# A fused RWKV scan and Sinkhorn MoE: the fallback becomes a loop over time steps, and its flag and branch move ahead of the decay table

## The chip, the cores and the metric

The kernel runs on one core of one Trainium2 chip. The metric is device time in microseconds (us), the median of several executions; lower is better. Engines are named as the profile names them: PE (TensorE matmul) and PEld (its weight load), DVE (VectorE), ACT (ScalarE), POOL (GpSimd) and SP (SyncE, which here only issues DMAs). A small q behind an engine's name means its sequencer, the part that reads instructions, waits for semaphores, branches and issues DMAs.

## What is computed

An attention-like recurrence with a decay per head and channel (B, H, S, D = 4, 8, 768, 48), whose output goes through a mixture of experts (3072 tokens, 384 wide, 8 experts of 1024) with gate weights that are normalised over rows and columns eight times. Cut to what matters:

```python
def _attn_ref(r, k, v, w, u):
    state = np.zeros((B, H, D, D), dtype=np.float32)
    for t in range(S):
        kt, vt, rt = (k[:, :, t], v[:, :, t], r[:, :, t])
        cur = np.einsum('bhd,bhe->bhde', u[None] * kt, vt)
        y[:, :, t] = np.einsum('bhd,bhde->bhe', rt, state + cur)
        state = w[None, :, :, None] * state + np.einsum('bhd,bhe->bhde', kt, vt)

def _moe_ref(x, w_gate, w1, w2):
    logits = x @ w_gate
    P = np.exp(logits - logits.max())
    for _ in range(8):
        P /= P.sum(1, keepdims=True) + 1e-09
        P /= P.sum(0, keepdims=True) + 1e-09
        P *= N / E
    for e in range(E):
        out += P[:, e:e + 1] * (np.maximum(x @ w1[e], 0.0) @ w2[e])
```

The decay w is drawn from 0.85 to 0.95.

## The kernel before

The scan is done in chunks of 128 time steps. Inside a chunk the powers of w are factored into r and k, so that a chunk is matmuls; a table of the powers (the decay table) is built once at the start. It works while w lies in [0.7, 1.1]. Channels outside of that are masked out of the table, and for them there is a fallback, scan_channels, which runs the recurrence channel by channel. Whether it runs is decided on the chip: a flag, the maximum over "w differs from w clamped", is loaded into a register of each engine (`nc.values_load`, L444), and an `If` (L445) jumps over the fallback when it is zero, as it is with the inputs above.

The program is fully unrolled, and the order on each engine is the order of the code: the wrapper `InOrder` (L21) keeps each engine's instructions as they are written, and records them all under L29, so groups in the profile are told apart by the tiles they write and read. The flag's load and the branch are not wrapped: where they fall among an engine's instructions is the framework's decision. Tiles of the pool `ps3` (L258, tag "pa") share four PSUM buffers in rotation: the fifth tile of the tag waits until the first is read out.

The start of the program, in order:

- w is loaded twice as `wt` (L264, L265; one half by SP, one by ACT's queue) for the table, and once as `wrow` (L266, ACT's queue) for the flag. SP loads r and k of token tiles 0 and 1 (`rn`, `kn`, L291).
- Fills: `hbx`, a third each on POOL, DVE and ACT (L305 to L313), then small ones on POOL.
- PE multiplies zeros (`spin`, tile `pz`) so that its clock is up when work comes: 25 matmuls (L314).
- DVE builds the decay table: `wsafe`, the scan `pw`, the flag's three instructions (L327 to L329), the reciprocal `iv`, two products `tab`. ACT copies two parts (`tabr`). PE transposes eight blocks (`pt_tab`, L342), and ACT copies them out as `rtab` and `ktab`. DVE writes `wc` and `wbd` from the table.
- The flag's load and the branch over the fallback.
- 8 more spins (L449). SP loads v of tile 0, `ub`, r and k of tile 2 (in the program as built these four stand ahead of SP's branch), then the first expert's weight w1 in three pieces (tile `ws`, L458), then tiles further on.

Behind that each token tile goes through prep (POOL: `rp` = rn times rtab; DVE: `kp` = kn times ktab), stage_b (transposes `prT`, `pkT` on PE, copies on ACT), stage_c (`pA` = kT by rT; DVE copies it under a mask to `at`; `pu`, from which DVE makes the state `S`), stage_d (`py`, then `x` on DVE) and the transposes and gate logits behind it. Five spins stand after stage_b and after stage_c while there is no expert work to put there. On DVE `wm`, the maximum of the first expert's w1 in three pieces, is placed among the tiles' instructions: its first piece stands between kp of tile 2 and `dg` and `at` of tile 0. From tile 5 on PE fills the gaps with the first expert's matmuls (`ph`, `po`), and from there to the end it is the experts that are computed.

The fallback before is a loop over the 4 batches (L384); in its body the 4 pairs of heads and 48 channel steps of each are unrolled. DVE's part of it is about 1,260 rows of the program, PE's about 1,620, SP's about 80.

## Time and profile before

| | |
|---|---|
| median of 3 runs | 1607.49 us (1604.43 to 1607.59) |
| the profiled execution's own time | 1602.74 us |
| its span on the core | 1601.0 us |
| PE busy | 1571.7 us, 98% |
| DVE, ACT, POOL busy | 1019.0, 668.6, 587.9 us |
| mean granted clock of PE | 0.995 |
| share of the chain that ended last on PE | 93% |
| PE busy in 0 to 10, 10 to 20, 20 to 30 us | 7.79, 3.79, 10.00 us |
| PE busy in 40 to 100 us, by tens | 9.32, 9.48, 8.46, 8.85, 7.70, 10.00 us |

The span runs from the first instruction on the core to the last; the execution's time has some 1.7 us around it. Busy time of PE counts the spins too, which compute nothing. In a row of the timeline stand the start, the duration, engine, line, operation, the tile written and the tiles read, how many instructions are merged, and in brackets how long the engine had stood idle and what released it.

### The profile page before, as it was taken

The page shows a single profiled execution, that of the slowest core. Times are in us where ns is not written, and L with a number is a line of the kernel's source. Part 1 is how long each engine was busy: PE and PEld are TensorE (multiplying, and loading weights), DVE is VectorE, ACT ScalarE, POOL GpSimd, SP SyncE. Part 2 cuts the span into 40 slices and gives each one's busy share as a digit, 9 for nine tenths or more (in the row PEclk, how much of TensorE's full clock was granted, in tenths as well). Part 3 has the DMA queues.
Part 4 walks back from the last instruction along what each step waited for, and adds up shares of the span by engine and source line. Part 5 has one row for each costly group of instructions (what it writes and reads, how often), then busy time and mean ns, then how long its engine had stood idle before and what let it go on. Part 6 is the DMA issues. An engine that isn't in the chain of part 4 may idle for free.

```text
span 1601.0 us, 24304 instructions
## 1 busy us (share of the span) xinstructions
PE 1571.7 (98%) x9433; PEld 909.6 (57%) x9433; DVE 1019.0 (64%) x1706; ACT 668.6 (42%) x1190; POOL 587.9 (37%) x688
## 2 busy tenths in 40 slices
PE   7999999999999999999999999999999999999999
PEld 5778777555455555555555555555555555555555
DVE  6776665675766666666666666666665666656554
ACT  2333333343444444454535454544444453535320
POOL 6567674442021343434243424243332424242200
PEclk8999999999999999999999999999999999999999
DMA  7333230212022567566666656664545554545434
GB/s 180 63 69 85 66 86 26 92 42 84 35 94 54 104 85 124 74 123 85 124 84 100 110 74 123 85 113 55 95 55 94 58 96 54 94 56 89 60 89 133
DMA packets 163899, 136.60 MB, mean 85 GB/s; under 512 B 88257, under 2 KB 158018, under 8 KB 163778
## 3 DMA queue, kind: packets, MB, share of 16 engines
q0 software_dynamic: 44928, 61.36, 31.6%
q1 hardware_dynamic: 118640, 73.63, 15.9%
q8 instruction: 75, 1.23, 0.3%
q14 instruction: 46, 0.38, 0.1%
q10 hardware_dynamic: 210, 0.00, 0.0%
HBM read 53.69 MB, written 80.22 MB: 84 GB/s over the span
## 4 chain that ended last, share of the span: by engine, by line
PE 93%; DVE 3%; POOL 1%; issue 1%; ACT 1%; ACTq 0%; DVEq 0%; POOLq 0%
PE po L29 46%; PE bZ L29 11%; PE bY L29 11%; PE ph L29 5%; PE bB L29 4%; PE bA L29 4%; PE py L29 4%; PE bC L29 2%; PE pA L29 1%; PE pu L29 1%; POOL tb L29 1%; PE pz L29 1%; PE prT L29 1%; PE pkT L29 1%; PE px L29 0%
## 5 line engine op out<-in xcount | busy, mean ns | idle before, releaser
L29 PE MATMUL po<-ws,hbx 128*128 128x384 f16 x3360 | 736.9, 326 | 0.0
L29 POOL DMA_DIRECT2D accd<-stg x288 | 250.4, 870 | 701.2 <-ACT stg L29 682.8
L29 PEld LDWEIGHTS <-hbx 128*128 128x128 f16 x3576 | 336.9, 98 | 287.4
L29 PEld LDWEIGHTS <-ws 128*128 128x128 f16 x3096 | 302.8, 98 | 248.2 <-issue 6.3
L29 ACT ACTIVATE hbx<-tb 128x512 f16<-128x512 f32 x224 | 141.5, 632 | 443.5 <-DVE tb L29 443.5
L29 PE MATMUL po<-ws,hb 128*128 128x384 f16 x1248 | 322.2, 327 | 3.2 <-DVE ws L29 2.3
L29 DVE TENSOR_TENSOR tb<-bY,tb 128x512 f32<-128x512 f32 x168 | 116.2, 692 | 194.4 <-PE bY L29 193.3
L29 ACT ACTIVATE stg<-po,pe 128x384 f32<-128x384 f32 x312 | 179.6, 575 | 128.0 <-PE po L29 102.5
L29 PE MATMUL bZ<-xv,ws 128*128 128x512 f16 x840 | 227.0, 379 | 0.7 <-DVE tb L29 0.6
L29 PE MATMUL bY<-xv,ws 128*128 128x512 f16 x840 | 227.0, 379 | 0.1
L29 DVE TENSOR_TENSOR tb<-bZ,tb 128x512 f32<-128x512 f32 x168 | 115.5, 688 | 132.9 <-PE bZ L29 132.9
L29 PEld LDWEIGHTS <-hb 128*128 128x128 f16 x1248 | 122.1, 98 | 96.4 <-issue 4.7
L29 POOL TENSOR_TENSOR ucb<-rawb 128x256 f32<-128x256 f32 x84 | 75.5, 949 | 93.1 <-DMA rawb<-in_moe_w_dram 66.7
L29 DVE TENSOR_TENSOR tb<-bB,tb 128x512 f32<-128x512 f32 x112 | 77.5, 692 | 49.6 <-PE bB L29 47.7
L29 PE MATMUL ph<-hbx,ws 128*128 128x384 f16 x576 | 103.9, 328 | 1.3 <-DVE hb L29 1.2
L29 DVE SCALAR_TENSOR_TENSOR hbx<-tb,hbx 128x512 f16<-128x512 f32 x112 | 78.0, 696 | 24.3 <-ACT hbx L29 19.5
L29 DVE SCALAR_TENSOR_TENSOR hb<-tb,hbx 128x512 f16<-128x512 f32 x112 | 77.2, 689 | 24.7 <-ACT hbx L29 19.5
L29 PE MATMUL bA<-xv,ws 128*128 128x512 f16 x336 | 90.8, 379 | 1.0 <-ACT tb L29 1.0
L29 PE MATMUL bB<-xv,ws 128*128 128x512 f16 x336 | 90.8, 379 | 0.0
L29 DVE SCALAR_TENSOR_TENSOR hb<-ph,hb 128x384 f16<-128x384 f32 x64 | 35.5, 555 | 59.0 <-ACT hb L29 58.8
L29 ACT COPY tb<-bZ 128x512 f32<-128x512 f32 x56 | 32.8, 586 | 68.1 <-PE bZ L29 68.1
L29 ACT ACTIVATE hb<-ph 128x384 f16<-128x384 f32 x64 | 31.5, 492 | 58.0 <-PE ph L29 56.7
(163 smaller groups left out, 1645.0 us busy)
## 6 DMA issues: line engine op xcount, KB each, us to landing
accd<-stg POOLq DMA_DIRECT2D x288, 192.0 KB, 3.7
rawb<-in_moe_w_dram SPq DMA_DIRECT2D x28, 768.0 KB, 7.3
e0d<-stg SPq DMA_DIRECT2D x48, 192.0 KB, 1.9
hb<-e0d SPq DMA_DIRECT2D x48, 192.0 KB, 3.5
rn<-in_r_dram SPq DMA_DIRECT2D x24, 192.0 KB, 3.1
kn<-in_k_dram SPq DMA_DIRECT2D x24, 192.0 KB, 3.5
vn<-in_v_dram SPq DMA_DIRECT2D x24, 192.0 KB, 2.8
accd<-stg SPq DMA_DIRECT2D x24, 192.0 KB, 1.8
```

Source lines behind the costliest of these rows:

```text
L29: return lambda *a, **k: self.tc.keep_in_program_order(f(*a, **k))
```

## The change

- The fallback becomes a short loop over the 768 time steps: it holds the state of 48 by 48 per batch and head with one partition per value channel, and each step is a handful of DVE instructions and seven DMAs. Its scratch tiles lie in `hbx` instead of `ws1`, `hb3` and PSUM. It has no PE instructions.
- The flag's load of w goes first on ACT's queue, its three DVE instructions stand right behind the fills and ahead of the table, and load and branch are written ahead of the table's code, without `high_priority`.
- The table's code (wsafe to wbd) stands behind SP's loads in the text. POOL's fills, mask and wbd, that followed it, stand before it.
- 25 spins before and 8 after the branch become 19 before it, 5 ahead of the table's transposes and 4 behind them.

```diff
+    wr = w.rearrange("(p two) d -> two d p", two=2)
+    S_.dma_start(wrow, w.rearrange("(o h) d -> o h d", o=1))
     V.memset(wt, 1.0)
-    wr = w.rearrange("(p two) d -> two d p", two=2)
     Q.dma_start(wt[:D, :], wr[0])
     S_.dma_start(wt[HP : HP + D, :], wr[1])
-    S_.dma_start(wrow, w.rearrange("(o h) d -> o h d", o=1))
...
-    spin(25)
-    wsafe = ac.tile([P, NPAIR], F32, name="wsafe")
...
-    V.tensor_scalar(wlim, wrow, W_MAX, W_MIN, op0=ALU.min, op1=ALU.max)
-    V.tensor_tensor(wlim, wlim, wrow, op=ALU.not_equal)
-    V.tensor_reduce(flag, wlim, axis=AX.XY, op=ALU.max)
-    V.reciprocal(iv, pw)
...
+    spin(19)
     wbd = ac.tile([P, NPAIR, 2, D], F32, name="wbd")
     G.memset(wbd, 0.0)
...
+    V.tensor_scalar(wlim, wrow, W_MAX, W_MIN, op0=ALU.min, op1=ALU.max)
+    V.tensor_tensor(wlim, wlim, wrow, op=ALU.not_equal)
+    V.tensor_reduce(flag, wlim, axis=AX.XY, op=ALU.max)
...
-        with tc.For_i(0, B, 1) as b:
-            for a in range(NPAIR):
...
-                for e in range(D):
...
+        with tc.For_i(0, S, 1) as t:
+            for dst, src in ((kb, k), (rb, r)):
+                Q.dma_start(
+                    dst,
+                    src.rearrange("b h s d -> s (b h) d")[bass.ds(t, 1)].broadcast_to([D, BH, D]),
+                )
+            Q.dma_start(vt, v.rearrange("b h s d -> s d (b h)")[bass.ds(t, 1)].rearrange("o d a -> (o d) a"))
+            V.tensor_tensor(rb, rb, stt, op=ALU.mult)
+            V.tensor_reduce(yv, rb, axis=AX.X, op=ALU.add)
...
+            V.tensor_tensor(of_b(stt), of_b(stt), for_b(wz), op=ALU.mult)
+            V.tensor_tensor(stt, stt, kv, op=ALU.add)
...
-    with tc.high_priority():
-        bad = nc.values_load(flag.bitcast(I32), min_val=0, max_val=0x3F800000)
-        with tc.If(bad > 0):
-            with tc.tile_pool(name="scratch", bufs=1, space=bass.MemoryType.DRAM) as scratch:
-                scan_channels(scratch)
-
-    spin(8)
+    bad = nc.values_load(flag.bitcast(I32), min_val=0, max_val=0x3F800000)
+    with tc.If(bad > 0):
+        with tc.tile_pool(name="scratch", bufs=1, space=bass.MemoryType.DRAM) as scratch:
+            scan_channels(scratch)
+
...
+    spin(5)
+    for src, dst in ((tab, rtab), (tabr, ktab)):
+        pt = ps3.tile([P, NPAIR, P], F32, tag="pa", name="pt_tab")
...
+        S_.copy(dst.rearrange("p a j d -> p a (j d)"), pt)
+    spin(4)
```

What this does to the order on the engines. On DVE, behind the last fill, with `hb_73` standing for the memory in which wrow, wlim, pw, iv and tab lie:

```order
+L29 TENSOR_SCALAR hb_73<-hb_73 1x384
+L29 TENSOR_TENSOR hb_73<-hb_73 1x384
+L29 TENSOR_REDUCE flag<-hb_73 1x1
+L384 TENSOR_LOAD flag
 L29 TENSOR_SCALAR wsafe<-wt 128x4
 L29 COPY hb_73<-wsafe 128x4x64
 L29 SCALAR_TENSOR_TENSOR hb_73<-hb_73 128x260
 L29 TENSOR_TENSOR good<-wt,wsafe 128x4
-L29 TENSOR_SCALAR hb_73<-hb_73 1x384
-L29 TENSOR_TENSOR hb_73<-hb_73 1x384
-L29 TENSOR_REDUCE flag<-hb_73 1x1
```

The flag's three instructions and the load of it moved from between good and the reciprocal to ahead of the whole table. The branch itself does not stand there: on DVE it falls between the two copies into wbd, behind the table.

On PE, from the table's transposes on; `pz` are the spins, and rows of L384 in the first and L362 in the second belong to the fallback's loop. Before:

```order
L29 MATMUL pt_tab<-ident,hb_73 128x128 x8
L444 TENSOR_LOAD flag
L445 COMPARE_AND_BRANCH
L384 COMPARE_AND_BRANCH
L384 UNCONDITIONAL_BRANCH x2
L1177 BRANCH_PREFETCH_HINT
L29 MATMUL pn_0_0_248<-ident,hb_73 96x128
```

and in the change:

```order
L29 MATMUL pt_tab<-ident,hb_73 128x128 x5
L385 COMPARE_AND_BRANCH
L362 COMPARE_AND_BRANCH
L362 UNCONDITIONAL_BRANCH x2
L1149 BRANCH_PREFETCH_HINT
L362 REGISTER_ALU
L362 COMPARE_AND_BRANCH
L362 UNCONDITIONAL_BRANCH
L385 UNCONDITIONAL_BRANCH x2
L29 MATMUL pt_tab<-ident,hb_73 128x128 x3
L29 LDWEIGHTS zeros
L29 MATMUL pz<-zeros 128x512
```

Before, the jump goes from behind the eighth transpose over some 1,620 rows of matmuls (the first is shown) to the spins. Now it stands between the fifth and the sixth transpose and goes over eight rows of loop control. Behind the four spins come prT and pkT of tile 0, as before.

On SP, the end of the fallback and what follows, in the change, with what each row waits for; `DMAHW` with a number is the semaphore of one of the eight lanes in which DMAs are counted, `hbx<-yd` is the fallback's last transfer:

```order
L29 DMA hbx<-yd 128x6x64 [waits DMAHW2_49]
L385 UNCONDITIONAL_BRANCH
L385 UNCONDITIONAL_BRANCH [waits DMAHW0_49,DMAHW1_49,DMAHW2_49,DMAHW3_49,DMAHW4_49,DMAHW5_49,DMAHW6_49,DMAHW7_49]
L29 DMA ws_74<-in_moe_w_dram 128x1024 [waits DMAHW3_49]
L29 DMA ws_74<-in_moe_w_dram 128x1024 [waits DMAHW4_49]
L29 DMA ws_74<-in_moe_w_dram 128x1024 [waits DMAHW5_49]
```

Nothing moved here: SP's loads of tiles 0 to 2 stand ahead of the branch in both, the same eight waits stand on the way past the fallback, and the first weight comes behind them. Only the fallback's own rows became fewer, about 40 instead of 80.

From prT of tile 0 on, all engines have the same instructions in the same order in both programs.

## The prediction

> **What bounds the kernel now.** I read the span first, then busy time by stage, then the timeline of the first 45 us.

> ```profile
> span 1601.0 us, 24304 instructions
> ```
> ```profile
> 10.00:20.00 10.00, 3.79 (x15) 1.88 (x16) 2.43 (x5) 1.07 (x2) 4.46 (x5) 0.63 0.56 131
> 20.00:30.00 10.00, 10.00 (x67) 7.34 (x67) 5.82 (x8) 3.33 (x6) 7.68 (x8) 0.86 1.02 250
> ```
> ```profile
> 100.00:200.00 100.00, 99.95 (x877) 79.24 (x876) 68.41 (x132) 32.93 (x67) 68.69 (x71) 1.00 0.35 79
> ```

> The columns are PE, PEld, DVE, ACT and POOL busy, then clock, DMA share and GB/s. From 100 us on PE has no room, and the program behind the branch is the same instruction for instruction. So the change is worth exactly what it moves the start of the attention tiles. PE works 3.79 us of the stretch 10 to 20, over two thirds of it padding. The cause is at the branch:

> ```profile
> 10.06 1.06 PE L29 MATMUL pt_tab<-ident,hb 128*128 128x128 f32 x8 [0.97 <-DVE wc L29]
> ...
> 11.39 1.95 POOL L29 TENSOR_TENSOR rp<-rn,rtab 128x384 f32<-128x384 f32 x2 [0.83 <-ACT rtab L29]
> ...
> 15.33 1.03 DVE L29 TENSOR_TENSOR kp<-kn,ktab 128x384 f32<-128x384 f32 x2 [4.38 <-DVEq L445]
> ...
> 17.23 1.98 SPq L29 DMA_DIRECT2D ws<-in_moe_w_dram  x3
> 17.28 3.57 PE L29 MATMUL pz<-zeros 128*128 128x512 f16 x8 [6.15 <-PEq L445]
> ...
> 20.64 1.06 PE L29 MATMUL prT<-ident,rp 128*128 128x128 f32 x4
> ```
> ```profile
> L445 POOLq COMPARE_BRANCH  x1: 45/45/45, 8.2 to 8.2; - x1
> ...
> L445 PEldq COMPARE_BRANCH  x1: 6429/6429/6429, 10.7 to 10.7; - x1
> ```

> The flag is zero, so every engine jumps over the fallback. POOL, which skips a handful of rows, takes 45 ns. PE, which skips some 1,600, takes 6.43 us, and then does 3.57 us of padding at half clock before tile 0's first transpose (prT) at 20.64. DVE, which skips some 1,260, stands 4.38 us. The length of the jump is the visible difference, and the DMA view has the code arriving:

> ```profile
> DMA  6679999899999988887677666545333332290000
> ...
> q8 instruction: 1, 0.02, 3.0%
> ```
> ```profile
> GB/s 0 0 0 0 0 0 0 0 0 0 0 137 6 6 9 9 0 0 0 0 0 0 0 0 0 0 0 0 0 0 0 0 0 0 0 0 0 0 0 0
> ...
> q1 hardware_dynamic: 13, 0.00, 1.1%
> ```

> The first two lines are 13 to 15 us, a column 0.05 us; the last two are 15 to 17.5, a column 0.0625 us. By 14.85 the loads of r, k, v and u have drained but for one DMA engine. There a 16 KB code packet took 3.0% of 16 engines for 2 us, 0.96 us, and 13 packets of a load sat behind it until 16.0. SP feels that:

> ```profile
> ub<-in_u_dram SPq DMA_DIRECT2D x1, 192.0 KB, 4.9
> rn<-in_r_dram SPq DMA_DIRECT2D x1, 192.0 KB, 5.0
> ```
> ```profile
> L445 SPq EVENT_SEMAPHORE  x2: 17/17/17, 13.8 to 14.6; - x2
> ```
> ```profile
> L445 SPq EVENT_SEMAPHORE  x5: 17/17/17, 16.8 to 17.1; - x5
> ```

> SP's path past the branch waits for its loads to land: ub (issued 8.90, in a row below, so 13.8), rn of tile 2 (9.53, so 14.5), and then kn of tile 2, seen at 16.8. Only then does ws, the first expert weight, go out at 17.23. Its 6.6 us are landings, not code.

> **The change, step by step.**

> ```profile
> 4.79 0.20 DVE L29 TENSOR_SCALAR wsafe<-wt 128x4 f32<-128x4 f32 x1
> ...
> 6.13 0.34 DVE L29 TENSOR_SCALAR hb<-hb 1x384 f32<-1x384 f32 x1
> ...
> 7.09 0.54 DVE L29 TENSOR_REDUCE flag<-hb 1x1 f32<-1x384 f32 x1
> 7.55 1.75 DVE L29 RECIPROCAL hb<-hb 128x260 f32<-128x260 f32 x1
> 8.42 0.35 POOL L29 MEMSET kp<- 128x128 f32 x2 [2.85 <-DVE flag L29]
> 8.49 0.37 SPq L29 DMA_DIRECT2D vn<-in_v_dram  x1
> ...
> 8.90 0.58 SPq L29 DMA_DIRECT2D ub<-in_u_dram  x1
> 9.24 0.68 DVE L29 TENSOR_TENSOR hb<-hb,good 128x256 f32<-128x256 f32 x2
> ...
> 9.53 0.43 SPq L29 DMA_DIRECT2D rn<-in_r_dram  x1
> ```
> ```profile
> L444 DVEq TENSOR_LOAD <-flag x1: 544/544/544, 10.2 to 10.2; - x1
> ```
> ```profile
> wt<-in_w_dram ACTq DMA_DIRECT2D x1, 0.8 KB, 2.2
> ```

> *Flag first.* Its three instructions run from 6.13 to 7.63, 1.50 us. They now stand where wsafe stood: 4.79 + 1.50 = 6.29, 1.34 earlier. The row of w that they read now heads ACT's queue; the nearest row is wt's, issued there at 0.99 and landed 2.2 us later, at 3.2, with 1.6 us of cover from the fills. If it came later than 4.79, each us late would be a us of flag.

> *Loads behind the flag.* SP issued vn 0.86 us after the flag; now 7.15. All four loads move by 1.34.

> *Decay table.* DVE does 4.79 to 9.92 less the flag's slot (6.13 to 7.55): 3.71 us, and 0.07 since the reciprocal now meets the end of the scan. Ahead of it DVE's sequencer waits for the flag and loads it (0.54): wsafe at 6.95, table at 10.73, 0.81 late. Queued behind that load are only the table's instructions, for which ACT's copies and PE's eight pt_tab wait: pt_tab 10.87, and POOL's rp, which waits for rtab, 12.2 to 13.2. POOL's fills come behind its own flag load, which ends 0.79 after the flag: 7.08. Those from 8.42 until 0.83 before 11.39 are 2.14 us; that leaves 3.0 before rp for mask's select and three small fills that stood ahead of the branch and ended by 5.57 with all the others. They are hidden; uncovered, they would delay rp by what is over 3.0. ACT's load of the flag hides behind DVE's scan.

> *Branch.* PE skips nine rows between its fifth and sixth pt_tab, DVE twenty, SP about forty. Between nothing and the 6.43 us of the long jump I take 0.05, by POOL's row, the nearest in length. The four spins behind pt_tab end at 13.0, under rp. So prT comes at 13.25, 7.4 earlier than 20.64. SP's waits for landings stay. What follows, as it is before:

> ```profile
> 20.58 3.34 SPq L29 DMA_DIRECT2D kn<-in_k_dram  x1
> ...
> 21.17 1.22 DVE L29 TENSOR_REDUCE wm<-ws 128x1 f32<-128x1024 f32 x1 [3.80 <-DMA ws<-in_moe_w_dram]
> ...
> 22.31 0.54 DVE L29 TENSOR_REDUCE dg<-rk 128x8 f32<-128x384 f32 x1
> ...
> 25.86 1.36 DVE L29 COPY_PREDICATED at<-mask,pA 128x512 f32<-128x512 int32 x2 [3.01 <-PE pA L29]
> ...
> 28.25 0.60 PE L29 MATMUL pkT<-ident,kp 128*128 128x128 f32 x4
> ...
> 32.28 0.54 DVE L29 TENSOR_TENSOR S<-pu,S 128x384 f32<-128x384 f32 x1
> ...
> 34.98 0.56 DVE L29 TENSOR_TENSOR x<-py,rk 128x384 f32<-128x384 f32 x1 [2.16 <-PE pmax_w L29]
> ```
> ```profile
> kn<-in_k_dram SPq DMA_DIRECT2D x1, 192.0 KB, 5.8
> ```
> ```profile
> 43.67 0.56 DVE L29 TENSOR_TENSOR x<-py,rk 128x384 f32<-128x384 f32 x1 [1.50 <-PE py L29]
> ```

> *What is late next: the weight load.* Without a 16 KB code packet in its way kn drains when its neighbours do, 14.85 − 1.34 = 13.5. Before, the last packet was through at 16.0 and SP saw it at 16.8, 0.8 later, and 0.43 after that came ws: 13.5 + 0.8 + 0.43 = 14.75, 2.5 earlier. ws landed 3.94 after its issue (21.17): 18.7. On DVE the reduction wm of ws stands ahead of dg and at; at starts 1.68 after wm (22.31 + 0.54): 20.37, its first half, 0.68, done at 21.05. PE is there by then: it needed 7.6 us from prT to tile 2's pkT, part of it at half clock, so at most until 20.9. And that pkT takes the PSUM buffer of the first pA (four buffers in rotation), which that half frees. So pkT goes from 28.25 to 21.05. From pkT to tile 0's x PE ran without a hole before, 6.73 us; x comes at 27.78 instead of 34.98. Beside it DVE took 6.96 from at to the end of S (25.86 to 32.82), so 20.4 to 27.3, in time; kn of tile 3, issued behind ws at 20.58 and landed 5.8 later, comes at 23.9 if it moves with ws, where DVE asks for it at about 24.5. From x to tile 1's x is again PE's own 8.69.

> **Sum:** 34.98 − 27.78 = **7.2 us**. The span goes to 1593.8 and the profiled execution from 1602.74 to 1595.5. That execution lies 4.75 under the runs' median of 1607.49; taken off the median, **1600.3**.

> *Unknowns.* If kn is as late after its issue as before, ws goes at 15.9 and the gain is 6.1. If SP sees kn together with rn (14.5 − 1.34 = 13.2), ws goes at 13.6 and at's half is done at 19.9: gain 8.3. The clock is the other: 0.63 in 10 to 20 and 0.86 in 20 to 30 is half speed for 7.4 and 2.8 us, so from 12.6 to 22.8, though PE had been idle for only 1.5 us at 12.6. The change has PE busy with pt_tab and spins from 10.87 to 13.0 and no hole over about 2 us, but the stretch before 12.6 is still half empty. The 7.6 us from prT to pkT had 2.2 at half speed, so they are 6.5 at full. With half speed until 19.5, 6.2 us of it, they end at 22.9: gain 5.4. With half speed all through, 13.0 us, pkT comes at 26.25: gain 2.0. I take full speed, since no hole like that from 11.1 to 17.28 is left; half speed all through is a rival.

> [...]

> **The rivals.**

> 1. *The weight load does not come earlier* (another landing or a code fetch holds SP until 17.2). For it: there are three waits in a row, each with a cause of its own. Against: the third is explained by one packet. wm stays at 21.17, at's first half ends at 23.53, pkT follows: gain 4.7, 1602.8.
> 2. *PE runs at half clock from prT to pkT*, as worked out: gain 2.0, 1605.5. For it: the drop at 12.6 before. Against: PE is then dense, and the clock was back 5.5 us after the work resumed at 17.28.
> 3. *The branch does not get cheaper*, since the 6.43 us were not the distance. PE then resumes at about 18.0; three pt_tab and four half-speed spins later prT starts at 20.1 against 20.64: gain 0.5, 1607.0. Against: POOL's 45 ns at the same branch, and the code packets.
> 4. *Slower:* the clock stays at half through tile 1's x. Then the 6.73 and 8.69 us behind pkT double too, 15.4 against rival 2's gain of 2.0: 13.4 slower, 1620.9. It decides once more than 2.0 us of that work runs at half speed, so if the clock is not back by about 30. For it, the padding that is cut (33 spins to 28) and the drop at 12.6; against, the row of 20 to 30, where such work brings the clock back.

> [...]

> **How the numbers follow.** Chances: forecast 0.66, rival 1 0.14, rival 2 0.07, rival 3 0.09, rival 4 0.04. The predicted time is the forecast's, 1600.3. The range leaves out rivals 3 and 4: up to rival 2, 1605.5; down to 1595.5, the best term of 8.3 (1599.2) with room for the runs, which spread over 3.2 us and have the profiled one 4.75 under the median. A measurement of this kernel tells about 0.2%, 3.2 us, from no change. Faster by more: forecast and rival 1, 0.80. Within: rivals 2 and 3, 0.16. Slower: rival 4, 0.04.

> **What would show it.** In the changed profile PE's branch should take under 0.2 us and DVE's kp follow its table without a wait for the branch; vn issue near 7.15, prT start near 13.3, ws issue near 14.75, wm start near 18.7, pkT of tile 2 start near 21.05, x come at 27.8 and 36.5; and from 100 us on each event should stand 7 us earlier than before. No code packet of 16 KB should fall among the loads before 15 us. ws at 17 shows rival 1, PEclk near 0.6 after 13 us rivals 2 or 4, a long COMPARE_BRANCH rival 3. A gain at x that is gone at 100 us would refute the first step, that the rest only follows.

## The result, and the profile after

| | before | after |
|---|---|---|
| median, runs of the first comparison | 1606.66 us (4 runs, 1604.43 to 1607.59) | 1597.34 us (4 runs, 1595.96 to 1598.19) |
| median, runs of a second comparison | 1602.48 us (15 runs, 1601.46 to 1606.14) | 1597.21 us (6 runs, 1593.85 to 1598.35) |
| the profiled execution's own time, its span | 1602.74, 1601.0 us | 1598.19, 1596.3 us |
| PE busy in 10 to 20 us | 3.79 us | 9.23 us |

The ratio after to before is 0.9943, 95% interval 0.9926 to 0.996, in the first comparison and 0.9964, 0.9951 to 0.9976, in the second. Faster, then, by 4 to 12 us, under one per cent. The forecast was 1600.3, in a range from 1595.5 to 1605.5; the median lies 3.0 under it.

First the branch. These are rows of the changed kernel's line of the `If` (L385): engine, operation, count, then the least, median and longest duration in ns, and when the first and last began.

```profile
L385 PEldq COMPARE_BRANCH  x1: 223/223/223, 10.8 to 10.8; - x1
L385 DVEq COMPARE_BRANCH  x1: 67/67/67, 10.8 to 10.8; - x1
```

PE's branch takes 0.22 us instead of 6.43, DVE's 0.07, and DVE goes on at 11.1 instead of standing 4.38 us. The timeline of PE shows what comes behind it:

```profile
12.14 1.91 PE L29 MATMUL pz<-zeros 128*128 128x512 f16 x4
13.85 0.97 PE L29 MATMUL prT<-ident,rp 128*128 128x128 f32 x4
...
20.71 0.60 PE L29 MATMUL pkT<-ident,kp 128*128 128x128 f32 x4
```

Tile 0's first transpose (prT) starts at 13.85 where it started at 20.64, and pkT of tile 2 at 20.71 where it was 28.25. The four padding matmuls took 1.91 us, where four took 1.03 at full clock in the second profile: they ran at half clock. SP and DVE:

```profile
14.22 1.29 SPq L29 DMA_DIRECT2D ws<-in_moe_w_dram  x3
```
```profile
18.01 1.22 DVE L29 TENSOR_REDUCE wm<-ws 128x1 f32<-128x1024 f32 x1 [1.85 <-DMA ws<-in_moe_w_dram]
...
19.61 1.35 DVE L29 COPY_PREDICATED at<-mask,pA 128x512 f32<-128x512 int32 x2
...
27.45 0.56 DVE L29 TENSOR_TENSOR x<-py,rk 128x384 f32<-128x384 f32 x1 [0.42 <-PE pmax_w L29]
...
36.13 0.56 DVE L29 TENSOR_TENSOR x<-py,rk 128x384 f32<-128x384 f32 x1
```

The first weight (ws) goes out at 14.22 instead of 17.23. DVE waited 1.85 us for it ahead of wm, and at follows 1.60 behind. This wait is not what ends last, though. The first half of at is done at about 20.3 (half of 1.35 us behind 19.61), and PE comes to tile 2's pkT, which needs the buffer that this half frees, only at 20.71. PE itself had no hole from 12.14 until past 39 us, as these rows show for two stretches (columns as in the prediction: PE, PEld, DVE, ACT, POOL busy, granted clock, DMA share, GB/s):

```profile
14.59:18.01 3.42, 3.42 (x33) 2.63 (x33) 1.57 (x2) 2.05 (x4) 3.34 (x4) 1.00 0.75 242
```
```profile
20.00:30.00 10.00, 10.00 (x87) 7.66 (x85) 9.11 (x20) 1.88 (x4) 8.25 (x10) 1.00 0.98 193
```

So after the change PE's own work from prT on sets the start of the tiles, with some 0.4 us to spare for the weight. Tile 0's x comes at 27.45 instead of 34.98, tile 1's at 36.13 instead of 43.67: **7.54 us**, forecast 7.2.

From there on the program is the same, but the 7.54 us do not last. A later x in DVE's timeline, before:

```profile
100.47 0.56 DVE L29 TENSOR_TENSOR x<-py,rk 128x384 f32<-128x384 f32 x1 [0.57 <-PE py L29]
```

and the same after:

```profile
95.22 0.56 DVE L29 TENSOR_TENSOR x<-py,rk 128x384 f32<-128x384 f32 x1 [0.57 <-PE py L29]
```

The lead is 5.25 us here (and 6.88 two tiles earlier, 75.75 against 68.87); at the end, by the spans, it is 4.7. The stretches of the changed kernel show why:

```profile
50.00:60.00 10.00, 9.20 (x67) 7.40 (x67) 9.12 (x20) 1.94 (x4) 5.73 (x6) 0.83 0.31 60
...
70.00:80.00 10.00, 7.71 (x59) 5.16 (x58) 7.67 (x17) 5.46 (x8) 5.28 (x5) 0.97 0.30 59
80.00:90.00 10.00, 10.00 (x82) 8.73 (x81) 5.93 (x12) 2.93 (x6) 3.38 (x3) 0.86 0.31 70
```

PE's clock was at half speed for a third of 50 to 60 (0.83) and for some 3.4 us about 80. Before had no such dip there in its profile. Whether these belong to the change is one question for the runs; which of the change's parts brought the 7.54 us is the other.

### The profile page after: what moved, and what is told of

Read it like the earlier page. It is cut to its first block, busy times and chain, and to the rows that moved or that the text cites. A ratio compares the mean times of both kernels' runs of the same rounds, so it can differ in the third digit from the quotient of the medians.

```text
span 1596.3 us, 24294 instructions
## 1 busy us (share of the span) xinstructions
PE 1571.7 (98%) x9428; PEld 911.1 (57%) x9428; DVE 1020.5 (64%) x1706; ACT 667.8 (42%) x1190; POOL 588.0 (37%) x688
## 3 DMA queue, kind: packets, MB, share of 16 engines
q1 hardware_dynamic: 118640, 73.63, 15.9%
## 4 chain that ended last, share of the span: by engine, by line
PE 92%; DVE 3%; POOL 1%; issue 1%; DMA 1%; ACT 1%; SPq 0%; ACTq 0%; POOLq 0%; DVEq 0%
PE po L29 46%; PE bZ L29 11%; PE bY L29 11%; PE ph L29 5%; PE bB L29 4%; PE bA L29 4%; PE py L29 4%; PE bC L29 2%; PE pA L29 1%; POOL tb L29 1%; PE pu L29 1%; PE prT L29 1%; PE pkT L29 0%; PE px L29 0%; DMA rn<-in_r_dram 0%
## 5 line engine op out<-in xcount | busy, mean ns | idle before, releaser
L29 PE MATMUL po<-ws,hbx 128*128 128x384 f16 x3360 | 736.9, 326 | 0.0
L29 POOL DMA_DIRECT2D accd<-stg x288 | 249.7, 868 | 701.7 <-ACT stg L29 682.8
L29 PEld LDWEIGHTS <-hbx 128*128 128x128 f16 x3576 | 337.1, 98 | 287.4
L29 PEld LDWEIGHTS <-ws 128*128 128x128 f16 x3096 | 302.8, 98 | 248.5 <-issue 6.5
L29 ACT ACTIVATE hbx<-tb 128x512 f16<-128x512 f32 x224 | 141.1, 630 | 444.9 <-DVE tb L29 444.9
L29 PE MATMUL po<-ws,hb 128*128 128x384 f16 x1248 | 322.9, 327 | 3.2 <-DVE ws L29 2.3
L29 DVE TENSOR_TENSOR tb<-bY,tb 128x512 f32<-128x512 f32 x168 | 116.2, 691 | 193.9 <-PE bY L29 193.9
L29 ACT ACTIVATE stg<-po,pe 128x384 f32<-128x384 f32 x312 | 179.4, 575 | 127.8 <-PE po L29 101.8
L29 PE MATMUL bZ<-xv,ws 128*128 128x512 f16 x840 | 227.0, 379 | 1.0 <-DVE tb L29 0.9
L29 PE MATMUL bY<-xv,ws 128*128 128x512 f16 x840 | 227.0, 379 | 0.0
L29 DVE TENSOR_TENSOR tb<-bZ,tb 128x512 f32<-128x512 f32 x168 | 115.5, 688 | 133.2 <-PE bZ L29 133.2
L29 PEld LDWEIGHTS <-hb 128*128 128x128 f16 x1248 | 122.2, 98 | 96.6 <-issue 5.0
L29 POOL TENSOR_TENSOR ucb<-rawb 128x256 f32<-128x256 f32 x84 | 75.4, 948 | 94.0 <-DMA rawb<-in_moe_w_dram 68.0
L29 DVE TENSOR_TENSOR tb<-bB,tb 128x512 f32<-128x512 f32 x112 | 77.4, 691 | 49.7 <-PE bB L29 47.8
L29 PE MATMUL ph<-hbx,ws 128*128 128x384 f16 x576 | 103.8, 328 | 1.2 <-DVE hb L29 1.2
L29 DVE SCALAR_TENSOR_TENSOR hbx<-tb,hbx 128x512 f16<-128x512 f32 x112 | 78.7, 703 | 24.2 <-ACT hbx L29 19.5
L29 DVE SCALAR_TENSOR_TENSOR hb<-tb,hbx 128x512 f16<-128x512 f32 x112 | 77.2, 689 | 24.6 <-ACT hbx L29 19.5
L29 PE MATMUL bA<-xv,ws 128*128 128x512 f16 x336 | 90.8, 379 | 1.0 <-ACT tb L29 1.0
L29 PE MATMUL bB<-xv,ws 128*128 128x512 f16 x336 | 90.8, 379 | 0.0
L29 DVE SCALAR_TENSOR_TENSOR hb<-ph,hb 128x384 f16<-128x384 f32 x64 | 35.5, 555 | 59.3 <-ACT hb L29 59.2
L29 ACT COPY tb<-bZ 128x512 f32<-128x512 f32 x56 | 32.8, 586 | 68.2 <-PE bZ L29 68.2
L29 ACT ACTIVATE hb<-ph 128x384 f16<-128x384 f32 x64 | 31.5, 492 | 57.9 <-PE ph L29 56.6
## 6 DMA issues: line engine op xcount, KB each, us to landing
accd<-stg POOLq DMA_DIRECT2D x288, 192.0 KB, 3.6
e0d<-stg SPq DMA_DIRECT2D x48, 192.0 KB, 2.1
hb<-e0d SPq DMA_DIRECT2D x48, 192.0 KB, 3.4
rn<-in_r_dram SPq DMA_DIRECT2D x24, 192.0 KB, 3.3
kn<-in_k_dram SPq DMA_DIRECT2D x24, 192.0 KB, 3.5
vn<-in_v_dram SPq DMA_DIRECT2D x24, 192.0 KB, 3.0
accd<-stg SPq DMA_DIRECT2D x24, 192.0 KB, 1.8
```

The source lines that it names most:

```text
L29: return lambda *a, **k: self.tc.keep_in_program_order(f(*a, **k))
```

## Experiments

All times below are of the slowest (here only) core. "x of tile 1" is the start of that DVE row; 43.67 before, 36.13 after.

### One part alone: the short fallback

The kernel before with the new body of the fallback; flag, branch, fills and padding written as before.

```diff
     def scan_channels(scratch):
-        with tc.For_i(0, B, 1) as b:
-            for a in range(NPAIR):
...
+        with tc.For_i(0, S, 1) as t:
...
```

> The kernel before with only the short fallback put in: flag, branch, fills and spins stand where they stood. Theory (the length of the jump and its code packets are the cost; the earlier flag is worth its own 1.34 us): PE's branch under 0.3 us, no 16 KB packet among the loads, ws issued near 15.6 us, x of tile 0 near 28.6, 1.1 behind the change's 27.45; time about 1601. Rival (the earlier flag and the branch's new place are what matters): ws near 17, x of tile 0 at 32 or later, time about 1605.

Measured: 1601.60 us (10 runs), ratio 0.999, interval 0.998 to 0.9999, against the kernel before. The jumps are short (PE 223 ns, DVE 67 ns), and yet x of tile 0 comes at 31.69, where 28.6 was expected, and x of tile 1 only at 40.38; ws, at 15.34, came as expected. POOL's timeline tells where the rest went:

```profile
8.22 0.20 POOL L29 MEMSET mask<- 128x128 f32 x1 [3.78 <-DVE flag L29]
11.45 0.99 POOL L29 TENSOR_TENSOR rp<-rn,rtab 128x384 f32<-128x384 f32 x1 [3.02 <-ACT rtab L29]
...
15.50 0.99 POOL L29 TENSOR_TENSOR rp<-rn,rtab 128x384 f32<-128x384 f32 x1
```
```profile
16.54 1.12 PE L29 MATMUL prT<-ident,rp 128*128 128x128 f32 x4 [2.24 <-POOL rp L29]
```

With another fallback the framework puts POOL's load of the flag ahead of the small fills, so that these, 3.1 us, now stand behind the first rp and ahead of the second, which starts at 15.50. PE waits 2.24 us for it, and its matmuls behind that run at half clock until pu at 22.47 (pkT of tile 1 takes 1.06 us and pA 1.97, where pkT of tile 0 ahead of the wait took 0.60 and pA in the change 1.16). The expectation that the short jump alone gives nearly all failed: by these rows the place of the fills takes away much of its gain. The run with the flag undone, below, bears on this.

### The change again

The changed kernel, unaltered, beside the same runs of before.

> The changed kernel once more. The step moved x of tile 1 by 7.5 us, the profiled executions differ by 4.7 and the medians by 9.3. Theory (7.5 us at the start, less 1.7 for each window of half clock that the profiled execution caught after 50 us and more or less of those in the others): x of tile 1 again near 36.1; the time between 1595 and 1600; the ratio near 0.9955. Rival (some other gain of 2 us in the steady part): a shift that grows after 100 us, ratio 0.994 or less.

Measured: 1597.21 us (1593.85 to 1598.35, 6 runs). This time the profiled execution is the fastest, 1593.85 us, and its mean granted clock is 0.999, where the first profile had 0.995.

```profile
13.16 0.66 PE L29 MATMUL prT<-ident,rp 128*128 128x128 f32 x4 [0.46 <-POOL rp L29]
```
```profile
17.55 1.22 DVE L29 TENSOR_REDUCE wm<-ws 128x1 f32<-128x1024 f32 x1 [1.48 <-DMA ws<-in_moe_w_dram]
...
35.58 0.56 DVE L29 TENSOR_TENSOR x<-py,rk 128x384 f32<-128x384 f32 x1
```

x of tile 1 is 8.09 us earlier than before. It is 0.55 earlier than in the first profile, where a half window had slowed pt_tab and the padding ahead of prT (1.57 and 1.91 us, here 1.06 and 1.03). Here too PE has no hole from tile 1's prT, at 14.44, until past 39 us, so that the weight is not what ends last (wm, at 17.55, came 0.46 earlier as well). By the spans, 1592.0 and 1601.0, the lead at the end is 9.0. A mean of 0.999 leaves room for about one half window in the whole run (an estimate: 0.1% of 1592 us is 1.6, and a window of 3.41 us at half clock loses 1.7), where the first profile had three before 83 us. So the dips at 55 and 80 are not part of the program, and without them the gain lasts.

### A long jump put back into the changed kernel, on PE, then on DVE

800 matmuls, and in the other run 1250 fills, that are never run are added to the fallback, ahead of its loop (the expectations of some later runs say in its body). No instruction that runs is changed.

```diff
         V.memset(stt, 0.0)
+        for n_ in range(0, 800, 50):
+            pq = ps2.tile([P, TB], F32, tag="po", name=f"pq_{n_}")
+            for _ in range(50):
+                T.matmul(pq, zeros[:, :P], zeros, start=True, stop=True)
```

```diff
         V.memset(stt, 0.0)
+        for _ in range(1250):
+            V.memset(kv, 0.0)
```

> The change with 800 matmuls that never run put into the fallback, so PE jumps over some 1,600 rows again; DVE's and SP's jumps stay short. The framework then puts PE's branch ahead of the table's transposes, at about 6.8 us, when the first loads have drained. Theory (a far jump waits for its code packet, and that waits behind loads): PE's branch takes 2 to 3.5 us there, hidden under the decay table, x of tile 0 within 0.3 us of 27.45. Rival (a far jump costs 6.4 us whatever the DMA engines do): PE is back at 13.3, prT at 17 or later, x of tile 0 near 30.9.

> The change with 1,250 fills that never run put into the fallback, so DVE alone jumps far again, at 10.8 us, in the midst of the loads. Theory: DVE stands about 4.3 us, kp starts near 15.3 instead of 13.0, and most of that is hidden, since wm waits for its weight at 18.0 anyway: x of tile 0 between 27.6 and 28.6. Rival (DVE's stall was what cost): x of tile 0 later by over 3 us, past 30.5.

Measured, PE: 1597.98 us (one run).

```profile
L389 PEldq COMPARE_BRANCH  x1: 3749/3749/3749, 6.9 to 6.9; - x1
```
```profile
10.78 1.24 PE L29 MATMUL pz<-zeros 128*128 128x512 f16 x5 [2.48 <-PEq L389]
11.86 1.04 PE L29 MATMUL pt_tab<-ident,hb 128*128 128x128 f32 x8
```

The branch takes 3.75 us, but the framework had put it at 6.9, among the padding, where PE would have waited for pt_tab's input, there at 10.78, anyway. Nearly all of the stall is hidden by that wait. What is not are the five padding matmuls behind the branch: they now start at 10.78, and pt_tab at 11.86 instead of 10.77. x of tile 0 comes at 27.94, 0.49 later than in the first profile of the change, where at most 0.3 was expected; x of tile 1 comes at 36.63, 1.05 later than in the second profile, whose clock was full there as it was here (the four spins behind pt_tab took 1.03 us in both). Lying in front of another wait, this long jump cost only what stuck out behind that wait, and padding made that about 1 us.

Measured, DVE: 1601.65 us (one run). The branch itself takes 67 ns; the stall stands behind it.

```profile
14.31 0.93 DVE L29 COPY wbd<-wc 48x192 f32<-48x192 f32 x1 [3.24 <-DVEq L387]
...
40.27 0.56 DVE L29 TENSOR_TENSOR x<-py,rk 128x384 f32<-128x384 f32 x1 [1.50 <-PE py L29]
```
```profile
16.66 0.66 PE L29 MATMUL pkT<-ident,kp 128*128 128x128 f32 x4 [1.84 <-DVE kp L29]
```

DVE stood 3.24 us, its kp came later, PE waited 1.84 us for it and ran from 18.0 to about 21.4 at half clock (five spins at 18.90 took 2.34 us, 1.24 at full clock), as it had ahead of prT (four took 1.91). x of tile 0 comes at 31.59, where 27.6 to 28.6 was expected, so the rival was right; x of tile 1 at 40.27, 4.1 later than in the changed kernel. In this profile the jump on DVE alone takes more than half of the gain at the start.

### The early flag undone

The changed kernel with the row of w loaded behind wt, the flag's instructions back behind `good`, and branch and loads behind the table. Short fallback and padding stay, and so does the place of the fills, which are marked `high_priority` for it.

```diff
-    V.tensor_scalar(wlim, wrow, W_MAX, W_MIN, op0=ALU.min, op1=ALU.max)
-    V.tensor_tensor(wlim, wlim, wrow, op=ALU.not_equal)
-    V.tensor_reduce(flag, wlim, axis=AX.XY, op=ALU.max)
...
     V.tensor_tensor(good, wt, wsafe, op=ALU.is_equal)
+    V.tensor_scalar(wlim, wrow, W_MAX, W_MIN, op0=ALU.min, op1=ALU.max)
+    V.tensor_tensor(wlim, wlim, wrow, op=ALU.not_equal)
+    V.tensor_reduce(flag, wlim, axis=AX.XY, op=ALU.max)
```

> The changed kernel with one part undone: the row of w for the flag is loaded behind wt again, the flag's three instructions stand behind 'good' again, and the branch with the loads behind it stands after the decay table. The short fallback stays, and POOL's fills stay ahead of the first rp, as in the changed kernel. Theory (the short jump gives nearly all, the early flag about its own 1.2 us): flag ends near 7.45, ws goes out near 15.3, wm near 18.9, x of tile 0 near 28.4 and of tile 1 near 37.0, that is 6.7 us earlier than before's 43.67; time 1 us above the changed kernel's in the same clock, 1595 to 1599. Rival (in the run with the short fallback alone the start stayed behind because the branch stood behind the table, not because POOL's fills stood behind the first rp): x of tile 0 stays near 31.7 and of tile 1 near 40.4.

Measured: 1598.30 us (9 runs, 1594.2 to 1599.3), ratio 0.9966, interval 0.9955 to 0.9978. The mean granted clock of the profiled run was 0.999.

```profile
15.24 1.29 SPq L29 DMA_DIRECT2D ws<-in_moe_w_dram  x3
```
```profile
21.30 0.66 PE L29 MATMUL pkT<-ident,kp 128*128 128x128 f32 x4 [1.88 <-DVE at L29]
```
```profile
28.09 0.56 DVE L29 TENSOR_TENSOR x<-py,rk 128x384 f32<-128x384 f32 x1 [0.18 <-PE pmax_w L29]
...
36.78 0.56 DVE L29 TENSOR_TENSOR x<-py,rk 128x384 f32<-128x384 f32 x1
```

ws and both x came within 0.4 us of the expectation. Here the weight does end last: PE waits 1.88 us ahead of tile 2's pkT for at, which stands behind wm. The change has 36.13 and, in its second profile, 35.58: the early flag is worth 0.65 to 1.2 us of the start, and 1 us in the medians, which is within their spread. The rival, that the branch behind the table was what held the run with the short fallback alone back, falls. This run and that one differ in POOL's order, in PE's padding, and in the half windows that came behind; which of the three counts most was not tried by itself.

### Long jumps put back behind the table: on PE, on DVE, on both

The kernel of the late flag with the same never-run additions, so that each long jump stands where it stood before the change.

> The kernel of the late flag, with 800 matmuls that are never run added to the body of the fallback's loop: PE's jump is long again and stands behind pt_tab, where it stood before the change; DVE's stays short. Theory (the code of a long jump is fetched through the same DMA engines as the loads, so that the jump costs PE its own stall and delays the load that SP waits for ahead of ws): PE's branch takes 3.7 us or more, prT starts at 15.5 to 18.5 instead of 12.26, a 16 KB code packet falls among the loads, ws goes out 1 to 2 us later than in the run with the late flag alone, and x of tile 1 comes at 39 to 42 instead of 36.78. Rival (PE's jump hides behind the weight load, and DVE's was what cost): x of tile 1 within 1 us of 36.78.

> The kernel of the late flag, with 1250 fills on DVE that are never run added to the body of the fallback's loop: DVE's jump is long again, PE's stays short. Theory: DVE stands 3.2 to 4.4 us at the branch, its three kp end near 17.5 instead of 15.3, wm starts near 19 and at near 21, so x of tile 1 at 37.5 to 39 with a full clock; as in the earlier run with the long jump on DVE, PE then has a hole ahead of pkT and may lose the clock for one or two windows of 3.4 us, up to 3.4 us more. Rival (DVE's jump is hidden behind the wait for ws): 36.8.

> The kernel of the late flag, with both additions: the jumps are long again on PE and on DVE, with the flag, the branch and the loads where they stood before the change; only the fallback's text and the fills differ from before. Theory (the length of the jumps is the whole of the gain but for about 1 us of the early flag): tile 1's x at 42 to 45 and the time 1601 to 1607, not to be told from the kernel before. Rival (something else in the change gives most of it): x of tile 1 below 40 and the time below 1600.

| | time | ratio to before, interval | x of tile 1 |
|---|---|---|---|
| late flag, short jumps | 1598.30 us | 0.9966 (0.9955 to 0.9978) | 36.78 |
| long on PE | 1603.94 us (8 runs) | 0.9999 (0.9984 to 1.0013) | 41.54 |
| long on DVE | 1601.32 us (8 runs) | 0.9977 (0.9963 to 0.9991) | 41.45 |
| long on both | 1602.46 us (10 runs) | 0.9989 (0.9975 to 1.0004) | 40.92 |

The run with the long jump on PE:

```profile
L424 PEldq COMPARE_BRANCH  x1: 5229/5229/5229, 10.7 to 10.7; - x1
```
```profile
16.09 1.09 PE L29 MATMUL prT<-ident,rp 128*128 128x128 f32 x4 [4.12 <-PEq L424]
```
```profile
21.16 0.38 PE L29 MATMUL pkT<-ident,kp 128*128 128x128 f32 x2 [1.85 <-issue]
```
```profile
q8 instruction: 1, 0.02, 2.8%
```

and on DVE:

```profile
15.26 0.99 DVE L29 COPY wbd<-wc 48x192 f32<-48x192 f32 x1 [5.00 <-DVEq L422]
```
```profile
17.57 1.12 PE L29 MATMUL pkT<-ident,kp 128*128 128x128 f32 x4 [4.66 <-DVE kp L29]
```

On PE the branch takes 5.23 us and a code packet of 16 KB falls among the loads (the row of 13 to 15 us); prT starts at 16.09 instead of 12.26. ws, expected 1 to 2 us later, goes out only 0.22 later, at 15.46. at then waits for pA and PE's own work ends last, so it is PE's own stall that counts here. Within pkT of tile 1 PE stood another 1.85 us for nothing that the profile shows, and this is in the 41.54 too. On DVE the stall is 5.00 us and PE waits 4.66 us for kp; 37.5 to 39 was expected for x of tile 1 at full clock, and up to 3.4 more with half clock, and PE ran at half clock from pkT at 17.57 (1.12 us) through the five spins at 20.18 (2.34 us, 1.24 at full clock). With both, 42 to 45 was expected, and it was 40.92. In these profiles the two stalls lie side by side: either alone puts x of tile 1 about as late as both.

In the times, code that is never run takes the gain away on PE: the median is that of the kernel before, and none of the eight runs is below 1600.1. With both jumps long the median is not to be told from before either; its interval just touches that of the short jumps, and three of the ten runs lie at 1597.9 to 1599.6. With the long jump on DVE alone some two thirds of the gain are left by the ratios (0.9977 against 0.9966), and the two intervals overlap: a loss is not shown. Three of its eight runs lie at 1597.2 to 1598.6, among those of the late flag with short jumps; the profiled one, 1602.45, is one of the five others.

### The padding behind the long jump

The kernel before with the 8 spins between fallback and prT taken out (L449).

```diff
-    spin(8)
```

> The kernel before with the 8 padding matmuls between the fallback and tile 0's first transpose taken out on PE, all else as before: long jumps, late flag, branch behind the table. Theory (of the 7.5 us by which tile 1's x came earlier, some 2 to 2.7 are the padding that stood behind the long jump and ran at half clock ahead of prT, 3.57 us in the profile of before): prT starts right when PE is past its jump, at 16 to 17.5 instead of 20.64, x of tile 1 comes at 40.7 to 42.5 instead of 43.67, time 1600 to 1603. Rival (the weight load, seen by SP at 17.2 and landed at 21.17, holds tile 0 anyway): x of tile 1 within 1 us of 43.67.

Measured: 1600.89 us (10 runs; the kernel before beside it 1603.30), ratio 0.9988, interval 0.9978 to 0.9997.

```profile
17.28 1.09 PE L29 MATMUL prT<-ident,rp 128*128 128x128 f32 x4 [6.16 <-DVE kp L29]
```
```profile
21.23 1.22 DVE L29 TENSOR_REDUCE wm<-ws 128x1 f32<-128x1024 f32 x1 [4.01 <-DMA ws<-in_moe_w_dram]
...
41.09 0.56 DVE L29 TENSOR_TENSOR x<-py,rk 128x384 f32<-128x384 f32 x1 [1.50 <-PE py L29]
```

prT starts as soon as the jump is over (the branch began at 10.7 and took 6.29 us), x of tile 1 comes at 41.09: in these two profiles 2.58 us of the start were padding that stood behind a stall. wm is as late as before (21.23), so the weight load was not yet what held tile 0 up.

### A shorter long jump

The changed kernel with 100 never-run matmuls instead of 800.

> The changed kernel with 100 matmuls that are never run added to the body of the fallback's loop, so that PE jumps over some 200 rows. Theory (what a jump costs follows from whether the code behind it has to be fetched, and so from its length): the branch takes between 0.22 us, as over nine rows, and 3.75 us, as over 800 matmuls; if the code is fetched in blocks larger than 200 rows, 0.2 us, if each jump past the fetched block costs a whole fetch, 2 to 4 us. The time stays within 0.2% of the changed kernel's either way, as the branch stands ahead of a wait for pt_tab's input. Rival (the wait was never for code): 0.2 us here, and the 3.75 us of the longer one were something else.

```profile
L389 PEldq COMPARE_BRANCH  x1: 361/361/361, 6.9 to 6.9; - x1
```

0.36 us over some 200 rows, against 0.22 over eight and 3.75 over some 1,600. The branch took longer the longer the jump, and little at this one, as the theory had it; whether that comes in steps, three points don't show, and the first of them was taken at another place (10.8 us, the others at 6.9). 1598.34 us (one run), x of tile 1 at 35.80.

### The holes filled

Padding moved to where PE is idle: 15 spins instead of 5 ahead of pt_tab and none behind it, and 6 ahead of tile 6's second expert product, in front of a hole of 2.29 us at 76.6.

```diff
-    spin(5)
+    spin(15)
...
-    spin(4)
...
+        if i == 6:
+            spin(6)
         run(2, i > 4)
```

> The changed kernel with padding moved and added on PE only: 15 padding matmuls ahead of pt_tab where 5 stood, none between pt_tab and prT where 4 stood, and 6 more ahead of tile 6's second expert product, where PE had a hole of 2.29 us at 76.6. Theory (a 3.4 us window in which PE is busy less than about 0.4 of the time gives half clock in the next one, and these two holes make such windows in some executions and not in others): the clock is full from 7 to 300 us but for at most one window near 55, prT starts near 13.2, x of tile 0 near 27.0 and of tile 1 near 35.6; the profiled run and the median lie at 1593.0 to 1595.5, the runs within 3 us of one another. Rival (the clock falls by itself, whatever PE does): half windows near 11, 55 or 79 remain, median near 1597.2 and spread 4.5 us as in the changed kernel.

Measured: 1595.51 us (5 runs, 1594.01 to 1596.43), ratio 0.9948, interval 0.993 to 0.9966; profiled run 1594.37 us. The two stretches that had been nearly empty:

```profile
9.62:13.03 3.41, 2.47 (x16) 1.45 (x14) 1.83 (x7) 1.48 (x3) 1.04 (x2) 1.00 0.86 143
...
74.47:77.88 3.41, 2.69 (x17) 1.49 (x16) 3.41 (x6) 1.05 (x2) 2.68 (x3) 1.00 0.00 0
```

The clock was 1.00 from 0 to 30, 50 to 90 and 100 to 200 us and 0.999 on the mean, as expected; but the mean was 0.999 in the second profile of the change too, so one profile does not show that the padding did it. The five runs spread over 2.4 us, the six of the change over 4.5. x of tile 0 and of tile 1 came at 27.38 and 36.06, 0.4 to 0.5 later than expected. The median is the lowest here, 1.7 us under the changed kernel's in the other comparison; the two ratios' intervals overlap, so that this is faster than before is shown, and that it beats the change is likely, not shown.

### The weight's maxima one tile later

The filled holes, and the first expert weight's maxima (wm) taken in tile 1's turn, with 2 spins instead of 5 at each place in the first five turns.

```diff
-            spin(5)
+            spin(2)
...
-        run(1, i > 4)
+        run(1, i > 4, i > 0)
```

> The kernel of the filled holes, and the maxima of the first expert weight (wm) not taken in tile 0's turn but in tile 1's, with 2 padding matmuls instead of 5 at each place in the first five turns. Theory (after the change the weight load is what ends last at the start, since wm stands ahead of at on DVE): at of tile 0 no longer waits for ws and comes 1.5 to 2.5 us earlier, x of tile 0 near 25 and of tile 1 near 33.5; time 1591 to 1593.5. Rival (another load, kn of tile 2 or 3, or POOL's products are as late): x of tile 0 27 or later, time 1593.5 to 1597; or the weight's split comes later and leaves a hole of 2 us or more on PE between 55 and 80 that takes the gain back: x of tile 1 at 33.5, but no gain at 100 us.

Measured: 1599.04 us (11 runs, 1597.17 to 1600.86), ratio 0.997, interval 0.996 to 0.9981: slower than with the holes filled alone.

```profile
17.57 1.36 DVE L29 COPY_PREDICATED at<-mask,pA 128x512 f32<-128x512 int32 x2
...
23.77 0.81 DVE L29 TENSOR_TENSOR kp<-kn,ktab 128x384 f32<-128x384 f32 x1 [4.41 <-DMA kn<-in_k_dram]
...
28.91 0.56 DVE L29 TENSOR_TENSOR x<-py,rk 128x384 f32<-128x384 f32 x1
```
```profile
48.90 1.16 PE L29 MATMUL pA<-rT,kT 64*128 64x128 f32 x14 [2.04 <-ACT rT L29]
```

at no longer waits for ws, and starts at 17.57 instead of 19.78; PE, with fewer spins, comes to tile 2's pkT at 18.99 instead of 20.58. But kn of tile 3 lands behind ws, and kp, ahead of wm on DVE, waits 4.41 us for it: x of tile 0 comes at 28.91, later than 27.38. The maxima are late in turn, which leaves holes on PE of 2.04 us ahead of 48.90 and of 1.98 ahead of 59.27, each followed by a half window (50.32 to 53.73 and 60.56 to 63.97, clock 0.50). The first rival was right, the next transfer in the same queue is as late; its 1593.5 to 1597 was too low all the same, since the holes that the second rival named (it put them at 55 to 80) came on top.

## Why the prediction was right, and where it was wrong

**The jumps: right, and shown for PE.** Never-run code put back on PE takes the gain in time away, and the branch's own row goes from 0.22 to 5.23 us with it. The sum had 0.05 for PE's short branch, by POOL's row, and it took 0.22. The step saw the stalls on PE and on DVE but summed PE's alone. In the profiles DVE's by itself holds x of tile 1 back as much (41.45 against 41.54), so there the gain at the start needed both; in the times of eight runs DVE's share is not shown.

**What the 7.54 us consist of.** 36.78 to 36.13 the early flag, 0.65 in this profile (1.2 by the second); 40.92 to 36.78 the jumps, 4.14; 43.67 to 40.92, 2.75, what else differs from before, of which the padding behind the jump was measured by itself as 2.58. Each of these is a difference of two single profiles whose half windows differ. The 4.14 is not the stall alone: in the run with both jumps long PE worked 6.08 us at half clock behind the stall (from prT at 16.05, 1.09 us, into pA at 21.77; the five spins between took 2.34 us, 1.24 at full clock), which is some 3 us more than at full clock (an estimate, half of the 6.08), while 1.88 us of the stall fall where PE waits for at when the jumps are short. The prediction had the padding inside "prT from 20.64 to 13.25" and didn't tell it apart.

**What ends last after the change: wrong.** The step let at, behind the weight, free pkT at 21.05 and had PE there by 20.9 at most. Measured, ws went out at 14.22 for 14.75, wm started at 18.01 for 18.7, the first half of at was done at about 20.3, and PE came at 20.71 without having waited. So the weight load came earlier, as forecast, and rival 1 is out, but it is PE's own work that ends last. That 20.71 and 21.05 lie so close is luck in part: two paths of nearly the same length were exchanged. As forecast, no code packet of 16 KB falls among the loads before 15 us. That such a packet had delayed ws by over 1 us is not borne out as a fixed price: with one among the loads ws went out at 17.23 before and at 15.46 in the run with the long jump on PE, 0.22 later than in that of the late flag alone.

**The clock from 12.6 on: wrong, at a cost of about half a us.** The step took full speed; it was at half (0.50) from 11.2 to 14.6, and prT came 0.60 late. Since PE's work ends last, this shifts what follows: x of tile 1 came 0.55 earlier in the second profile, whose clock was full. The weight would have allowed some 0.4 us of it in the first.

**The first step, that the rest only follows: failed in the profiled run.** "From 100 us on each event should stand 7 us earlier" is 5.25 there, and 8.1 for the same instruction in the second profile. The program behind is the same; what differs is in which executions PE's small holes between 50 and 85 us cost a half window. The forecast took the clock for a matter of the start alone.

**The size of the total.** The forecast took 7.2 off the median of three runs, 1607.49. Later medians of before, of 13 to 25 runs, are 1602.48 to 1603.61, and that of the change is 1597.21. Against the median taken beside it, 1602.48, this is a gain of 5.3 us, and 6.4 against the highest of those medians. So two terms were mis-sized: the gain that lasts, 1 to 2 us less than 7.2 in the middle of many executions, and the starting point, some 4 us too high in the three runs there were. The second outweighs the first, which leaves the 3.0 on the low side; that the two errors point in opposite ways is luck. The prediction saw that the profiled execution lay 4.75 under the median. It did not say why; in the second comparison the slowest runs of before, 1605.8 and 1606.1 us, had mean granted clocks of 0.993 and 0.991 and those near 1602.3 had 0.995 or 0.996, so the clock is the likely cause.

Rivals 2 and 4 (half clock through the start) did not happen in either profile of the change: its half windows at the start were one of 3.4 us or none. Rival 3 is out by the branch's row.

## What to carry to other kernels

Code that is never run is not free where it is jumped over: the more of it there was on PE, the longer PE's branch took (0.22, 0.36, 3.75 us), and DVE stood 3.24 and 5.00 us for its own. Where two engines jump far, look at both: in these profiles a long jump on either one held the start up about as much as on both (x of tile 1 at 41.54 and 41.45, and at 40.92). Look at what stands behind a stall in an engine's order, padding above all: written to bridge the stall, it added 2.58 us to it here. And in a program that is bound by PE, a gain at the start should be followed to the end in more than one profile, since half windows of the clock can take back a good part of what such a change brings (here 7.5 us at the start, 4.7 at the end of one profile and 9.0 of the other).

## What the runs showed of the hardware

```profile
7.77:11.18 3.41, 0.78 (x6) 0.44 (x5) 3.18 (x7) 0.81 (x2) 2.22 (x5) 1.00 0.71 129
11.18:14.59 3.41, 3.41 (x15) 2.33 (x13) 1.84 (x3) 1.17 (x2) 2.39 (x3) 0.50 0.50 106
...
52.14:55.55 3.41, 2.61 (x24) 2.39 (x22) 3.41 (x6) 0.48 (x1) 2.94 (x4) 1.00 0.00 0
55.55:58.96 3.41, 3.41 (x25) 2.85 (x25) 2.61 (x9) 0.42 (x1) 2.64 (x3) 0.50 0.29 58
76.03:79.44 3.41, 1.12 (x8) 0.56 (x7) 3.28 (x5) 0.12 (x1) 3.33 (x3) 1.00 0.00 0
```

and of its second:

```profile
9.09:12.51 3.42, 1.73 (x12) 1.22 (x12) 2.12 (x6) 1.48 (x3) 1.29 (x3) 1.00 0.87 170
```

The hole ahead of pt_tab takes 2.63 of 3.41 us of one window in the first (0.78 us busy, 23%, then half clock). In the second it is 1.98 us long, begins before the window and shares it with 1.73 us of work (51%, full clock).

Of the windows before from 5.84 to 111.65 us, and after from 4.36 to 110.17, that ran at full clock, three had PE busy for 23 to 33% of the time (1.06, 0.78 and 1.12 us), and all three were followed by half clock; 53 had PE busy for 58% or more, and of these one was, the one from 52.14 above with 2.61 us, where before's from 67.28 with 2.62 us was not. In other runs 1.12 us (33%, with 100 never-run matmuls, from 75.44) and twice 42% (1.42 and 1.43 us, with the later maxima, from 46.91 and 57.15) were followed by half clock, and once 42% was not (1.42 us, second profile of the change, from 73.95). Why the one of 2.61 us was followed by half clock and the last one was not stays unexplained.

So a window that was idle for 58% of its time (1.42 of 3.41 us busy) was enough in one run. This fits the drop 1.5 us into the hole of before, which the prediction saw: the window from 9.25 to 12.66 had PE busy for 1.06 us.

**It did not always come back after one busy window.** In the run with 100 never-run matmuls the clock stayed at half (0.50) for three windows, from 78.86 to 89.10, in which PE was never idle. The first and the last of them:

```profile
78.86:82.27 3.41, 3.41 (x20) 3.41 (x17) 0.56 (x1) 0.96 (x2) 0.00 (x0) 0.50 0.00 0
...
85.68:89.10 3.42, 3.42 (x13) 1.67 (x11) 2.84 (x6) 1.57 (x3) 2.41 (x2) 0.50 0.98 218
```

x of tile 1 had come 0.22 us behind that of the second profile of the change, and the run ends 4.5 behind it (spans 1596.5 and 1592.0). Why the clock stayed down, no run tells.

**The far jump had no one price.** PE's branch over some 1,600 rows took 3.75 us at 6.9, 5.19 and 5.23 at 10.7, and 6.29 and 6.43 there in the kernels with the old fallback. Over some 200 rows it took 0.36 us, over eight 0.22. What set the size of the wait over the same length, such as the load on the DMA engines, was not tried by itself.
